# Linear attention and an MLP on one core: windows 3 to 5 back to chunks of 128, and a reordered beginning

## The chip, the cores and the metric

The kernel runs on one core of a Trainium2 chip. The metric is the device time of one execution in microseconds; the time before is the median of three runs, 218.67 us (218.31 to 218.92). The profile is of one such execution; its span, from the first to the last instruction, is 216.7 us.

## The reference

Inputs are q, k and v of shape (batch 4, heads 8, sequence 768, head size 64), one decay factor per head (lam, between 0.97 and 0.99), a LayerNorm weight of 512 and two MLP weights, 512 x 2048 and 2048 x 512, all in float32. Decaying linear attention is followed by an MLP with a residual:

```python
for b in range(nb):                                   # blocks of 64 positions
    intra = einsum('bhic,bhjc->bhij', qb, kb) * Dmask # Dmask = lam**(i-j) for i >= j, else 0
    intra = einsum('bhij,bhjd->bhid', intra, vb)
    inter = einsum('bhid,bhde->bhie', qb * lam_pow, kv_state)
    out[:, :, sl] = intra + inter
    kv_state = lam_block * kv_state + einsum('bhsd,bhse->bhde', kb * rev_pow, vb)
x  = out, heads side by side                          # (4, 768, 512)
xn = (x - mean) / sqrt(var + 1e-6) * g_ln
result = x + relu(xn @ w_ch1) @ w_ch2
```

The block of the reference is only a way to compute it: any block length gives the same values.

## The kernel before

Work goes in 12 windows of 256 positions; window u is batch u % 4, third u // 4 of the sequence. Each window has two halves of 128 rows (`ab`), and makes one group of 256 rows for the MLP: eight steps of the first product (`m1`, 8 matmuls of 256 columns each), then eight of the second (`m2`, 4 of 512 columns). TensorE takes the attention of later windows between these steps.

q is scaled by powers of lam and v by inverse powers, so that a plain 0/1 mask stands for the decay within a chunk. The constant LB parts the windows in two kinds. Below LB a chunk has 128 positions; two neighbouring positions lie on one partition, so that a load has rows of 512 bytes. From LB on a chunk has 64 positions, rows have 256 bytes, and a load is two transfers:

```python
    XB = 3
    LB = 3
    ...
    def source(src, u, hs):
        cc, b = divmod(u, B)
        return src[b, hs, cc * W:(cc + 1) * W, :].rearrange("h (p j) d -> p h (j d)", j=2)

    def fill(got, name, u, hs):
        src = dict(k=k, q=q, v=v)[name]
        if u < LB:
            nc.sync.dma_start(got[:, hs], source(src, u, hs))
            return
        cc, b = divmod(u, B)
        for j in range(2):
            nc.sync.dma_start(got[:, hs, j * D:(j + 1) * D],
                              src[b, hs, cc * W + j * C:cc * W + (j + 1) * C, :].rearrange("h p d -> p h d"))
```

The attention of a window in chunks of 128: `kv` (32 matmuls of 64 columns, the state's new terms), `scores` (two halves of 16 matmuls of 128 columns), `mask`, `av` (64 matmuls of 64 columns), `inter` (up to twice 16 matmuls with the carried state). In chunks of 64: `kv64` (32), `scores64` (32 of 64 columns), `mask64` (half as many elements), `av64` (32), `inter` as above, and two more sums for the states in between.

```python
    def scores(u, hf, early=False):
        ...                                      # sc: two PSUM tiles, of tag "mm" if early, else of tag "sc" (2 buffers)
        for i in range(2):
            for jk in range(2):
                for ab in range(2):
                    for e in range(2):
                        nc.tensor.matmul(sc[e][half[ab], i, jk, :], lhsT=kT[half[e], 2 * hf + i, jk, half[ab]],
                                         rhs=qT[half[e], 2 * hf + i, :, half[ab]], ...)

    def av(u, pairs, chunks=(0, 1)):
        ...
        for p in pairs:
            for e in range(2):
                for j in range(2):
                    for jq in range(2):
                        for ab in chunks:
                            nc.tensor.matmul(s["po"][ab][half[jq], 2 * p + e, :],
                                             lhsT=s[f"mA{p // 2}"][half[ab], e, p % 2, j, half[jq]],
                                             rhs=s["vb"][half[ab], 2 * p + e, j], ...)

    def av64(u):
        ...
        for p in range(NP):
            for e in range(2):
                for j in range(2):
                    for ab in range(2):
                        nc.tensor.matmul(s["po"][ab][half[j], 2 * p + e, :], lhsT=s["mA"][half[ab], e, p, j],
                                         rhs=s["vb"][half[ab], 2 * p + e, j], ...)

    def mask_by_act(u, hf):                      # ScalarE copies the scores out, VectorE multiplies by the mask
        for e in range(2):
            nc.scalar.copy(s[f"mA{hf}"][:, e], s[f"sc{hf}"][e])
        ...
```

The transposed keys and queries of windows 0 to 2 come from TensorE (`transpose_pe`, copied out of PSUM by ScalarE or VectorE), those of later windows from the DMA (`transpose_dma`, on the sync queue); so it is with x^T, the MLP's input (`to_xT`). The sync queue issues in program order, and all loads, transposes and nearly all stores are on it.

The beginning, up to the first MLP tile:

```python
    lam_b = const.tile([128, H], F32)
    nc.scalar.dma_start(lam_b, lam[None, :].to_broadcast([128, H]))
    load_window(0, parts=2)
    nc.scalar.dma_start(g_one, moe_g_ln[None, :])
    ...
    g_all = ps.tile([128, DM], F32, tag="po1", name="g_all")
    nc.tensor.matmul(g_all, lhsT=ones, rhs=g_one, start=True, stop=True)   # spreads the LayerNorm weight
    nc.scalar.activation(lnlam, lam_b, ACT.Ln)
    nc.scalar.activation(lam_q[:, :, 0], lnlam, ACT.Exp, scale=e_q)
    ...
    in_k(0, nc.vector, HA)
    transpose_pe(0, 0, (0, 1))
    keep_busy(1, "po0")                                                    # one filler matmul
    ...                                                                    # Exp: lam_v (2), lam_s (2), lam_p (2)
    in_q(0, nc.vector, HA)
    ...
    transpose_pe(0, 1, (0, 1))
    transpose_pe(0, 0, (2, 3), nc.vector)
    nc.scalar.copy(g_row, g_all)
    transpose_pe(0, 1, (2, 3))
    ...
    scores(0, 0)
    mask(0, 0)
    scores(0, 1, early=True)
    mask_by_act(0, 1)
    kv(0)
    ...                                          # state, av, inter, norm of window 0
    transpose_pe(1, 0, (0, 1), nc.vector)
    transpose_pe(1, 0, (2, 3), nc.vector)
    to_xT(0, 0)
    inter(0, 1)
    norm(0, 1, early=True)
    m1a.tile(0, 0)                               # first MLP tile
    to_xT(0, 1)
    ...
```

The later part is a list of MLP steps (`plan`), with attention steps hung behind given numbers; step 22 is the first of group 2, and a group has 16 steps (38 is the first of group 3, 54 of group 4, 70 of group 5):

```python
    add(11, (open_window, 3), (in_k, 3, nc.scalar), (in_q, 3, nc.gpsimd))
    add(12, (s4, 2), (make_keep64,), (in_v, 3, nc.gpsimd))
    add(12, (transpose_dma, 3, 0), (to_xT, 2, 0), (transpose_dma, 3, 1), (to_xT, 2, 1))
    for name in "kqv":
        add(12, (load_one, 4, name))
    ...
    add(22, (load_one, 5, "k"))
    add(22, (first64, 3))                        # kv64, scores64, masks and states of window 3
    add(26, (transpose_dma, 4, 0), (transpose_dma, 4, 1), (load_one, 5, "q"))
    add(28, (wind_up, 3), (p4, 3), (load_one, 5, "v"))
    add(32, (first64, 4))
    ...
    for j in range(5, NU):
        at = 55 + 16 * (j - 6)
        ...
        add(at + 2, (X, j), (p4, j - 1))         # rest of window j - 1, first half of window j
```

Of the kernel before, what the change touches and what calls it, by code (L numbers as in the profile page):

```python
# [16 lines left out]
def kernel(  # L17
# [11 lines left out]
    nc = tc.nc  # L29
# [23 lines left out]

    half = [slice(0, 64), slice(64, 128)]
    XB = 3
    LB = 3

    def mm_tile(shape, dtype, name):
        return ps.tile(shape, dtype, tag="mm", bufs=4, name=name)
# [43 lines left out]
    def load_w2(c):  # L103
        nc.gpsimd.dma_start(w2[c], moe_w_ch2[c * W2K * 128:(c + 1) * W2K * 128, :].rearrange("(k p) d -> p k d", p=128))

    lam_b = const.tile([128, H], F32)
    nc.scalar.dma_start(lam_b, lam[None, :].to_broadcast([128, H]))
    load_window(0, parts=2)
# [38 lines left out]
    eps_t = const.tile([128, 1], F32)  # L147
    nc.vector.memset(eps_t, eps)

    e_q = const.tile([128, 1], F32)  # L150
    nc.vector.tensor_copy(e_q, io_i)
    nc.vector.tensor_scalar(e_q[half[1]], e_q[half[1]], float(-C), None, op0=ALU.add)
# [7 lines left out]

    ones = const.tile([1, 128], F32)
    nc.vector.memset(ones, 1.0)
    g_all = ps.tile([128, DM], F32, tag="po1", name="g_all")
    nc.tensor.matmul(g_all, lhsT=ones, rhs=g_one, start=True, stop=True)  # L164

    lnlam = const.tile([128, H], F32)
    nc.scalar.activation(lnlam, lam_b, ACT.Ln)
    lam_q = const.tile([128, H, 2], F32)
# [26 lines left out]
    def in_k(u, eng, hs=ALL):  # L195
        src = qkv_in[u]["k"][:, hs].rearrange("p (a e) j d -> p a e j d", e=2)
        dst = part(0, st[u]["kq"], hs)
        for j in range(2):
            (eng.copy if eng is nc.scalar else eng.tensor_copy)(dst[:, :, :, j], src[:, :, :, j])  # L199
# [27 lines left out]
    def transpose_dma(u, a):  # L227
        s = st[u]
        if "kqT" not in s:
            s["kqT"] = wk.tile([128, 2, NP, 2, 128], BF16, tag="kqT", bufs=3, name="kqT")  # L230
        nc.sync.dma_start_transpose(s["kqT"][:, a].rearrange("p b j t -> p (b j) t"),
                                    s["kq"][:, a].rearrange("p b j e d -> p (b j e d)"))

    def scores(u, hf, early=False):

# [24 lines left out]
    def mask_by_act(u, hf):  # L260

        s = st[u]
        for e in range(2):
            nc.scalar.copy(s[f"mA{hf}"][:, e], s[f"sc{hf}"][e])
        kp = keep_h.rearrange("p a b t -> p a (b t)")
        for e in range(2):
            m = s[f"mA{hf}"][:, e]
            nc.vector.tensor_tensor(m, m, kp[:, None, :, :].to_broadcast([128, 2, 2, 128]), op=ALU.mult)

    def kv(u, tag="mm"):  # L270

# [170 lines left out]
    def to_xT(u, ab):  # L442
        s = st[u]
        t = 2 * u + ab
        g = group_of[t]
        i = t - groups[g][0]
        if i == 0:
            xT_of[g] = gp.tile([128, KA, GT * 128], BF16, tag="xT", bufs=3, name="xT")
        dst = xT_of[g][:, :, i * 128:(i + 1) * 128]
        if u >= 2:  # L450
            nc.sync.dma_start_transpose(dst, s["xc"][:, ab])
        else:
            xt = mm_tile([128, KA, 128], BF16, "xt")
# [145 lines left out]
    nc.vector.tensor_copy(e_p[:, 0:1], io_p)  # L599
    nc.vector.tensor_scalar(e_p[:, 1:2], e_p[:, 0:1], -1.0, None, op0=ALU.mult)  # L600
    for i in range(2):
        nc.scalar.activation(lam_p[:, i], lnlam, ACT.Exp, scale=e_p[:, i:i + 1])
    in_q(0, nc.vector, HA)
    behind(qkv_in[0]["k"][:, 0, 0, 0:1])
    load_w1(0)
# [9 lines left out]
    scores(0, 0)  # L615
# [40 lines left out]
    transpose_pe(1, 1, (2, 3))  # L656
# [45 lines left out]
    def first64(u):  # L702
        kv64(u)
        scores64(u)
        mask64(u, 0)
        states64(u, 0)
        mask64(u, 1)
        states64(u, 1)

    def s0(u):  # L710
        kv(u, "po")
# [15 lines left out]
    def wind_up(u):  # L727


        s = st[u]  # L730
        if u < LB:
            av(u, range(NP))
        else:
            av64(u)
        inter(u, 0, fence=False)
        qT = s["kqT"][:, 1]
        has = [s["S"][ab][1] is not None for ab in range(2)]
        rest = [ps.tile([128, H, D], F32, tag="sc", bufs=2, name=f"rest{ab}") if has[ab] else None for ab in range(2)]
# [3 lines that stand above are left out]
                    ab = 1 - e  # L742
                    if s["S"][ab][jq] is not None:
                        nc.tensor.matmul(rest[ab][half[jq], 2 * p + e, :], lhsT=qT[half[e], p, jq, half[ab]],
                                         rhs=s["S"][ab][jq][half[e], p, :],
                                         start=(p == 0), stop=(p == NP - 1), skip_group_check=True)
        s["x"] = xp.tile([128, 2, DM], F32, tag="x", name="x")
        s["mv"] = xp.tile([128, 2, 2], F32, tag="mv", name="mv")
        s["xc"] = wk.tile([128, 2, DM], BF16, tag="xc", name="xc")
        for ab in range(2):  # L750
            x, xh = s["x"][:, ab], s["x"][:, ab].rearrange("p (a e d) -> p a e d", e=2, d=D)
            nc.scalar.copy(x, s["po"][ab].rearrange("p h d -> p (h d)"))
            if has[ab]:

                odd = xh[:, :, 1 - ab]
                rows = slice(0, 128) if s["S"][ab][0] is not None else half[1]
                nc.vector.tensor_tensor(odd[rows], odd[rows], rest[ab].rearrange("p (a e) d -> p a e d", e=2)[rows, :, 1 - ab], op=ALU.add)
# [100 lines left out]
    add(6, (s2, 2))  # L858
    add(8, (s0, 2))
    add(10, (s3, 2))  # L860
    add(11, (open_window, 3), (in_k, 3, nc.scalar), (in_q, 3, nc.gpsimd))
    add(12, (s4, 2), (make_keep64,), (in_v, 3, nc.gpsimd))
    add(12, (transpose_dma, 3, 0), (to_xT, 2, 0), (transpose_dma, 3, 1), (to_xT, 2, 1))
    for name in "kqv":
        add(12, (load_one, 4, name))
    add(15, (rstd_of, 2))
    add(22, (load_one, 5, "k"))
    add(22, (first64, 3))
    add(23, (open_window, 4), (in_q, 4, nc.gpsimd), (in_v, 4, nc.gpsimd))
    add(25, (in_k, 4, nc.vector))  # L870
    add(26, (transpose_dma, 4, 0), (transpose_dma, 4, 1), (load_one, 5, "q"))
    add(28, (wind_up, 3), (p4, 3), (load_one, 5, "v"))
    add(28, (open_window, 5), (in_k, 5, nc.gpsimd))
    add(32, (first64, 4))
    add(32, (in_q, 5, nc.gpsimd), (in_v, 5, nc.gpsimd))
    add(34, (rstd_of, 3), (transpose_dma, 5, 0), (transpose_dma, 5, 1))
    for j in range(5, NU):
        at = 55 + 16 * (j - 6)
        if j > 5:
            for n, name in zip((20, 19, 18) if j == 6 else (23, 21, 19), "kqv"):  # L880
                add(at - n, (load_one, j, name))
            add(at - 13, (p0, j))
            add(at - 8, (transpose_dma, j, 0), (transpose_dma, j, 1))
        add(at + 2, (X, j), (p4, j - 1))
        add(at + 9, (rstd_of, j - 1))
    add(151, (wind_up, NU - 1), (p4, NU - 1))
    add(159, (rstd_of, NU - 1))
# [32 lines left out]
```

## Time and profile before

| | before |
|---|---|
| time, median of 3 | 218.67 us |
| span in the profile | 216.7 us |
| TensorE clock granted, mean of the span | 0.991 |
| DMA: bytes moved, mean rate | 37.13 MB, 171 GB/s |
| packets under 512 bytes, of all | 86961 of 103502 |

Times in the profile are microseconds from the span's start. PE is TensorE's matmuls, PEld its weight loads, DVE VectorE, ACT ScalarE, POOL GpSimd, SP the sync engine; a q behind a name means that engine's DMA issues. L484 is line 484 of the kernel: L484 is the first MLP product, L522 the second, L327 `scores64`, L164 the spread of the LayerNorm weight. TensorE's matmuls overlap, so a single one's duration is longer than the distance to the next: the rate is read from how long a run of them takes. An "issue" wait is one for which the profile shows no releaser.

### The profile page before, as it was taken

To read this page: it belongs to the slowest core of one execution; us is meant where nothing else is said; L and a number is where in the kernel's file an instruction comes from. 1 tells how busy PE (TensorE), PEld (TensorE's weight loads), DVE (VectorE), ACT (ScalarE), POOL (GpSimd) and SP (SyncE) were. 2 spreads that over 40 slices of the span, in tenths; PEclk is the share of its full clock that TensorE was granted. 3 is DMA by queue.
4 is the path that set the end of the run, shared out by engine and by line. 5 is a ranking of instruction groups with operands and counts; after the bars stand their busy time and mean duration, and the time that the engine had idled before them with its cause. 6 is when DMAs were issued, how large, how long until landed. Compare 5 with 4: busy or idle time off the path is not lost.

```text
span 216.7 us, 6491 instructions
## 1 busy us (share of the span) xinstructions
PE 199.6 (92%) x2796; PEld 137.4 (63%) x2811; DVE 102.5 (47%) x226; ACT 87.7 (40%) x167; POOL 81.1 (37%) x116
## 2 busy tenths in 40 slices
PE   2989899999991999999998999999999999999992
PEld 0468688444861486586575585684784874865862
DVE  2678452464852629338247246266174192532011
ACT  4766678140550046064063063262360460641610
POOL 4749049053372558418219129037055020000000
PEclk9999999999999799999999999999999999999999
DMA  4999999997989999999898799999987611320304
GB/s 122 291 271 209 225 267 167 224 208 150 211 256 220 154 222 238 197 176 228 166 221 196 145 235 182 147 219 208 208 194 150 146 23 32 101 48 0 100 0 97
DMA packets 103502, 37.13 MB, mean 171 GB/s; under 512 B 86961, under 2 KB 100529, under 8 KB 103474
## 3 DMA queue, kind: packets, MB, share of 16 engines
q1 hardware_dynamic: 98944, 32.39, 73.8%
q0 software_dynamic: 4224, 4.19, 12.1%
q8 instruction: 22, 0.36, 0.8%
q10 hardware_dynamic: 306, 0.14, 0.3%
q14 instruction: 6, 0.05, 0.1%
HBM read 27.27 MB, written 6.29 MB: 155 GB/s over the span
## 4 chain that ended last, share of the span: by engine, by line
PE 83%; DMA 5%; ACT 3%; DVE 3%; issue 2%; SPq 1%; POOL 0%; ACTq 0%
PE pm L522 36%; PE pm L484 34%; DMA kin<-in_k_dram 2%; PE pm1t L496 2%; PE pm2h L513 2%; DMA kqT<-kq 1%; PE sc L327 1%; PE po L380 1%; SPq L550 1%; DMA g_one<-in_moe_g_ln_dram 1%; PE po L406 1%; PE pk L346 1%; PE tp L224 1%; PE g_all L164 1%; ACT kqT L225 1%
## 5 line engine op out<-in xcount | busy, mean ns | idle before, releaser
L487 ACT ACTIVATE hT<-pm 128x512 bf16<-128x512 f32 x92 | 55.0, 601 | 94.0 <-PE pm L484 94.0
L484 PE MATMUL pm<-xT,w 128*128 128x256 bf16 x736 | 85.6, 273 | 1.0 <-issue 1.0
L522 PE MATMUL pm<-w,hT 128*128 128x512 bf16 x353 | 81.9, 382 | 1.2 <-issue 0.5
L484 PEld LDWEIGHTS <-w 128*128 128x128 bf16 x736 | 70.3, 98 | 12.4 <-issue 1.2
L522 PEld LDWEIGHTS <-hT 128*128 128x128 bf16 x368 | 35.8, 99 | 41.0 <-issue 1.4
L543 DVE SCALAR_TENSOR_TENSOR o<-pm,rstd,x 128x512 f32<-128x512 f32 x23 | 17.3, 750 | 48.1 <-PE pm L522 47.9
L287 POOL TENSOR_TENSOR Sn<-Stmp,lam_s 128x256 bf16<-128x256 f32 x17 | 10.5, 620 | 67.4 <-DVE Stmp L365 62.4
L210 POOL TENSOR_TENSOR kq<-qin,lam_p 128x512 bf16<-128x512 f32 x18 | 18.4, 1046 | 2.1 <-ACT kq L199 2.1
L216 POOL TENSOR_TENSOR vb<-vin,lam_p 128x1024 bf16<-128x1024 f32 x9 | 17.1, 1898 | 4.3 <-DMA vin<-in_v_dram 4.1
L435 DVE SCALAR_TENSOR_TENSOR xc<-po,mv,g_row 128x512 bf16<-128x512 f32 (+1 forms) x22 | 15.3, 701 | 1.7
L333 DVE TENSOR_TENSOR mA<-sc,keep 128x512 bf16<-128x512 f32 x18 | 12.3, 681 | 5.0 <-PE sc L327 5.0
L417 DVE COPY seen<-po 128x8 f32<-128x8 f32 x17 | 2.2, 161 | 25.5 <-PE po L406 25.5
L428 ACT COPY x<-po 128x512 f32<-128x512 f32 x16 | 8.7, 588 | 10.9 <-PE po L406 5.6
L430 DVE BATCH_NORM_STATS2 stats<-x 128x6 f32<-128x512 f32 x16 | 11.0, 684 | 0.8 <-ACT x L428 0.8
L199 POOL CAST kq<-kin 128x512 bf16<-128x512 f32 (+1 forms) x16 | 9.2, 603 | 4.2 <-DMA kin<-in_k_dram 4.2
L327 PE MATMUL sc<-kqT 64*64 64x64 bf16 x288 | 4.6, 199 | 4.7 <-DMA kqT<-kq 4.7
L362 DVE TENSOR_TENSOR Smid<-pk,Sn 128x256 f32<-128x256 f32 x17 | 7.2, 424 | 1.7
L257 DVE TENSOR_TENSOR mA<-sc,keep 128x512 bf16<-128x512 f32 x8 | 5.2, 686 | 5.6 <-PE sc L247 5.6
L370 POOL CAST Sm<-Smid 128x256 bf16<-128x256 f32 x18 | 7.4, 410 | 1.0 <-DVE Smid L362 1.0
L406 PE MATMUL po<-Sn,kqT 64*64 64x64 bf16 x172 | 7.0, 199 | 0.0
L327 PEld LDWEIGHTS <-kqT 64*64 64x64 bf16 x288 | 3.7, 111 | 4.8 <-issue 4.8
L365 DVE TENSOR_TENSOR Stmp<-pk,Smid 128x256 f32<-128x256 f32 x14 | 5.9, 424 | 0.7
(99 smaller groups left out, 152.8 us busy)
## 6 DMA issues: line engine op xcount, KB each, us to landing
out_dram<-o SPq DMA_DIRECT2D x22, 256.0 KB, 4.7
kin<-in_k_dram SPq DMA_DIRECT2D x20, 256.0 KB, 4.3
qin<-in_q_dram SPq DMA_DIRECT2D x20, 256.0 KB, 5.4
vin<-in_v_dram SPq DMA_DIRECT2D x20, 256.0 KB, 5.2
w<-in_moe_w_ch_dram POOLq DMA_DIRECT2D x8, 512.0 KB, 8.8
kin<-in_k_dram SPq DMA_DIRECT2D x2, 512.0 KB, 6.5
qin<-in_q_dram SPq DMA_DIRECT2D x2, 512.0 KB, 8.9
vin<-in_v_dram SPq DMA_DIRECT2D x2, 512.0 KB, 9.1
```

What stands on the lines that cost most here:

```text
L199: (eng.copy if eng is nc.scalar else eng.tensor_copy)(dst[:, :, :, j], src[:, :, :, j])
L210: eng.tensor_tensor(dst[:, :, :, j], src[:, :, :, j], lq[:, :, :, j:j + 1].to_broadcast([128, n, 2, D]), op=ALU.mult)
L216: eng.tensor_tensor(st[u]["vb"][:, hs], qkv_in[u]["v"][:, hs], lv.to_broadcast([128, n, 2, D]), op=ALU.mult)
L287: eng.tensor_tensor(dst, src, lam_s[:, :, None].to_broadcast([128, NP, D]), op=ALU.mult)
L327: nc.tensor.matmul(s["sc"][e][half[ab], p, j, :], lhsT=kT[half[e], p, j, half[ab]], rhs=qT[half[e], p, j, half[ab]], start=(p == 0 and j = ...
L333: nc.vector.tensor_tensor(s["mA"][:, e], s["sc"][e], keep64[:, None, None, :].to_broadcast([128, NP, 2, D]), op=ALU.mult)
L430: nc.vector.bn_stats(stats, po if early else x)
L435: nc.vector.scalar_tensor_tensor(xc[:, sl], in0=po[:, sl], scalar=mv[:, 0:1], in1=g_row[:, sl], op0=ALU.subtract, op1=ALU.mult)
L484: nc.tensor.matmul(pm[:, b, :], lhsT=w1[n // W2K][:, kk, (n % W2K) * 128:(n % W2K + 1) * 128], rhs=xT_of[g][:, kk, 0:N], start=(b == 0 and ...
L487: nc.scalar.activation(hT[:, u * NB:(u + 1) * NB, 0:N], pm, ACT.Relu)
L522: nc.tensor.matmul(acc[i], lhsT=hT[:, kk, i * 128:(i + 1) * 128], rhs=w2[kk // W2K][:, kk % W2K, :], start=(kk == 0), stop=(kk == KB - 1))
L543: nc.vector.scalar_tensor_tensor(o[:, ab], in0=a, scalar=rstd[:, ab:ab + 1], in1=x[:, ab], op0=ALU.mult, op1=ALU.add)
```

## The change

It does two things. Windows 3 to 5 are computed in chunks of 128 again (LB is 6 instead of 3), with their own placement in the step list: window 4 is loaded right behind window 3, window 5 some steps later, and each window's attention is spread over four places. This gives loads with longer rows, and other times for loads, transposes and the attention's matmuls.

The beginning is reordered: one activation table with logarithm and exponential is loaded at the start instead of two at first use; the exponentials run one after the other; the LayerNorm weight is spread after the first key transposes, and the filler matmul is left out; the second half of window 0's mask is split between VectorE and ScalarE; the first x^T is built in two PSUM banks, copied out by two engines; and window 1's key transposes stand behind the first MLP tile.

```diff
-    LB = 3
+    LB = 6
...
+    nc.scalar.preload_act_table_set("natural_log_exp_and_others")
     lam_b = const.tile([128, H], F32)
     nc.scalar.dma_start(lam_b, lam[None, :].to_broadcast([128, H]))
...
-    g_all = ps.tile([128, DM], F32, tag="po1", name="g_all")
-    nc.tensor.matmul(g_all, lhsT=ones, rhs=g_one, start=True, stop=True)
...
+    def mask_two_ways(u, hf):
+        s = st[u]
+        m = s[f"mA{hf}"][:, 1]
+        nc.scalar.copy(m, s[f"sc{hf}"][1])
+        mask(u, hf, (0,))
+        kp = keep_h.rearrange("p a b t -> p a (b t)")
+        nc.vector.tensor_tensor(m, m, kp[:, None, :, :].to_broadcast([128, 2, 2, 128]), op=ALU.mult)
...
-            xt = mm_tile([128, KA, 128], BF16, "xt")
-            for kk in range(KA):
-                nc.tensor.transpose(xt[:, kk, :], s["xc"][:, ab, kk * 128:(kk + 1) * 128], ident)
-            nc.scalar.copy(dst, xt)
+            n_x = 2 if t == 0 else 1
+            for i_x in range(n_x):
+                w = KA // n_x
+                xt = mm_tile([128, w, 128], BF16, "xt")
+                for kk in range(w):
+                    at = i_x * w + kk
+                    nc.tensor.transpose(xt[:, kk, :], s["xc"][:, ab, at * 128:(at + 1) * 128], ident)
+                (nc.vector.tensor_copy if i_x else nc.scalar.copy)(dst[:, i_x * w:(i_x + 1) * w], xt)
...
-    in_k(0, nc.vector, HA)
-    transpose_pe(0, 0, (0, 1))
-    keep_busy(1, "po0")
     for j in range(2):
         nc.scalar.activation(lam_v[:, :, j], lnlam, ACT.Exp, scale=e_v[:, j:j + 1])
     ...                                          # lam_s
+    in_k(0, nc.vector, HA)
+    transpose_pe(0, 0, (0, 1))
+    g_all = ps.tile([128, DM], F32, tag="po1", name="g_all")
+    nc.tensor.matmul(g_all, lhsT=ones, rhs=g_one, start=True, stop=True)
...
     transpose_pe(0, 1, (0, 1))
     transpose_pe(0, 0, (2, 3), nc.vector)
+    scores(0, 0)
+    transpose_pe(0, 1, (2, 3))
     nc.scalar.copy(g_row, g_all)
-    transpose_pe(0, 1, (2, 3))
+    for i in range(2):
+        nc.scalar.activation(lam_p[:, i], lnlam, ACT.Exp, scale=e_p[:, i:i + 1])
...
-    mask_by_act(0, 1)
+    mask_two_ways(0, 1)
...
-    transpose_pe(1, 0, (0, 1), nc.vector)
-    transpose_pe(1, 0, (2, 3), nc.vector)
     to_xT(0, 0)
     inter(0, 1)
     norm(0, 1, early=True)
     st[0]["tmp"] = state_sum(0, 1)
     m1a.tile(0, 0)
+    transpose_pe(1, 0, (0, 1), nc.vector)
+    transpose_pe(1, 0, (2, 3), nc.vector)
     to_xT(0, 1)
...
     load_window(3, after_pool=True)
+    load_window(4)
...
+    add(12, (s4, 2), (p4, 2), (p0, 3, nc.vector), (transpose_dma, 3))
+    for n, name in zip((14, 15, 16), "kqv"):
+        add(n, (load_one, 5, name))
+    add(17, (p0, 4))
+    add(25, (s1, 3))                              # s1: kv, scores half 0, states, masks
+    add(25, (transpose_dma, 4))
+    add(27, (s2, 3))                              # s2: scores half 1, masks
+    add(28, (p0, 5))                              # p0: k, q and v of a window to bf16, scaled
+    add(29, (s3, 3))                              # s3: av, first carry
+    add(30, (s4, 3), (p4, 3))                     # s4: second carry, norm; p4: x^T by DMA
+    for n, name in zip((30, 31, 32), "kqv"):
+        add(n, (load_one, 6, name))
...
+    add(37, (transpose_dma, 5))
+    add(38, (s1, 4))
+    add(39, (p0, 6))
+    add(40, (s2, 4))
+    add(42, (s3, 4))
+    add(44, (s4, 4), (p4, 4))
+    add(46, (transpose_dma, 6))
+    add(50, (s1, 5), (rstd_of, 4))
+    add(53, (s2, 5))
...
+            if j == 6:
+                add(at + 1, (X1, j))              # rest of window 5, states of window 6
+                add(at + 5, (X2, j), (p4, j - 1)) # scores and masks of window 6, end of window 5
+            else:
                 add(at + 2, (X, j), (p4, j - 1))
```

More of the change, by code (lines that the diff above doesn't have):

```diff
@@ L148 @@
     nc.vector.memset(eps_t, eps)
+    nc.vector.tensor_copy(e_p[:, 0:1], io_p)
+    nc.vector.tensor_scalar(e_p[:, 1:2], e_p[:, 0:1], -1.0, None, op0=ALU.mult)
     e_q = const.tile([128, 1], F32)
@@ L225, in transpose_pe, with transpose_dma @@
         (eng.tensor_copy if eng else nc.scalar.copy)(s["kqT"][:, a, pairs[0]:pairs[0] + n], tp)
-    def transpose_dma(u, a):
+    def transpose_dma(u):
         s = st[u]
[L229 to L232, printed above, removed]
+        s["kqT"] = wk.tile([128, 2, NP, 2, 128], BF16, tag="kqT", bufs=3, name="kqT")
+        for a in range(2):
+            nc.sync.dma_start_transpose(s["kqT"][:, a].rearrange("p b j t -> p (b j) t"),
+                                        s["kq"][:, a].rearrange("p b j e d -> p (b j e d)"))
     def scores(u, hf, early=False):
@@ L597 @@
         nc.scalar.activation(lam_s[half[e]], ln_p[half[e], :, e], ACT.Exp, scale=float(C))
+    in_k(0, nc.vector, HA)
+    transpose_pe(0, 0, (0, 1))
+    g_all = ps.tile([128, DM], F32, tag="po1", name="g_all")
+    nc.tensor.matmul(g_all, lhsT=ones, rhs=g_one, start=True, stop=True)
     nc.vector.tensor_tensor(lam_q[:, :, 1], lam_q[:, :, 0], lam_b, op=ALU.mult)
[L599 to L602, printed above, removed]
     in_q(0, nc.vector, HA)
@@ L614 @@
     in_v(0, nc.gpsimd, HB)
-    scores(0, 0)
     mask(0, 0)
     scores(0, 1, early=True)
-    mask_by_act(0, 1)
+    mask_two_ways(0, 1)
     kv(0)
@@ L700, in p0 @@
         in_v(u, nc.gpsimd)
[L702 to L708, printed above, removed]
     def s0(u):
@@ L755, in wind_up @@
                 odd = xh[:, :, 1 - ab]
-                rows = slice(0, 128) if s["S"][ab][0] is not None else half[1]
-                nc.vector.tensor_tensor(odd[rows], odd[rows], rest[ab].rearrange("p (a e) d -> p a e d", e=2)[rows, :, 1 - ab], op=ALU.add)
+                nc.vector.tensor_tensor(odd, odd, rest[ab].rearrange("p (a e) d -> p a e d", e=2)[:, :, 1 - ab], op=ALU.add)
             stats = wk.tile([128, 6], F32, tag="stats", name="stats")
@@ L860 @@
     add(10, (s3, 2))
[L861 to L865, printed above, removed]
-    add(15, (rstd_of, 2))
[L867 to L877, printed above, removed]
+    add(12, (s4, 2), (p4, 2), (p0, 3, nc.vector), (transpose_dma, 3))
+    for n, name in zip((14, 15, 16), "kqv"):
+        add(n, (load_one, 5, name))
@@ new lines @@
+    add(15, (rstd_of, 2))
+    add(17, (p0, 4))
[7 more added lines that the diff above has]
+        add(n, (load_one, 6, name))
+    add(34, (rstd_of, 3), (make_keep64,))
+    add(37, (transpose_dma, 5))
[5 more added lines that the diff above has]
+    add(46, (transpose_dma, 6))
@@ L878 @@
+    add(50, (s1, 5), (rstd_of, 4))
+    add(53, (s2, 5))
+    for j in range(6, NU):
         at = 55 + 16 * (j - 6)
-        if j > 5:
-            for n, name in zip((20, 19, 18) if j == 6 else (23, 21, 19), "kqv"):
+        if j > 6:
+            for n, name in zip((23, 21, 19), "kqv"):
                 add(at - n, (load_one, j, name))
             add(at - 13, (p0, j))
-            add(at - 8, (transpose_dma, j, 0), (transpose_dma, j, 1))
-        add(at + 2, (X, j), (p4, j - 1))
+            add(at - 8, (transpose_dma, j))
+        if j < LB:
+            add(at, (s1_s3, j))
+            add(at + 4, (s2_s4, j), (p4, j - 1))
+        else:
+            if j == 6:
+                add(at + 1, (X1, j))
+                add(at + 5, (X2, j), (p4, j - 1))
+            else:
+                add(at + 2, (X, j), (p4, j - 1))
```

## The prediction

> **What bounds the kernel now.** I read the busy shares first, then the chain that ended last, then TensorE's waits, then stretches cut where the chain changes, then the timelines of the sync queue and of ScalarE. The first line says that TensorE is the bound, and the second, the engines' shares of the chain, agrees:
>
> ```profile
> PE 199.6 (92%) x2796; PEld 137.4 (63%) x2811; DVE 102.5 (47%) x226; ACT 87.7 (40%) x167; POOL 81.1 (37%) x116
> ...
> PE 83%; DMA 5%; ACT 3%; DVE 3%; issue 2%; SPq 1%; POOL 0%; ACTq 0%
> ```
>
> So only two things can move the time: matmul work, and the 17.1 us (216.7 - 199.6) in which TensorE stands still. TensorE's waits (engine, line, releaser: sum, times, longest in us) name most of that idle time:
>
> ```profile
> PE sc L327 <- DMA kqT<-kq: 4.7, 1, 4.7
> PE g_all L164 <- DMA g_one<-in_moe_g_ln_dram: 4.1, 1, 4.1
> PE pm L484 <- issue: 1.0, 1, 1.0
> PE po L393 <- issue: 0.7, 1, 0.7
> ```
>
> The second is the wait for the first data. The first is one hole in mid-kernel. Stretches (start:end, length; busy us of the engines; granted clock, DMA share, GB/s) place it. The four below are window 2 with the second products of groups 0 and 1, then the stages of groups 2, 3 and 4:
>
> ```profile
> 37.86:53.83 15.97, 15.65 (x191) 7.47 (x193) 8.43 (x17) 3.10 (x6) 5.22 (x8) 1.00 1.01 192
> 53.83:76.16 22.33, 17.21 (x281) 11.50 (x281) 12.72 (x25) 6.05 (x11) 10.57 (x15) 0.92 1.06 212
> 76.16:91.52 15.36, 15.31 (x225) 10.47 (x225) 7.77 (x17) 6.05 (x11) 9.48 (x11) 1.00 1.08 218
> 91.52:106.88 15.36, 15.31 (x225) 10.46 (x225) 7.76 (x17) 6.05 (x11) 6.93 (x9) 1.00 1.03 191
> ```
>
> Group 2's stage takes 22.33 us, a normal one 15.36. The timelines of the sync queue (start, duration) and of TensorE, one after the other, show why:
>
> ```profile
> 58.60 3.32 SPq L550 DMA_DIRECT2D out_dram<-o  x4
> 61.96 2.39 SPq L75 DMA_DIRECT2D kin<-in_k_dram  x2
> 64.46 3.49 SPq L231 DMA_TRANSPOSE kqT<-kq  x2
> ...
> 70.00 0.65 PE L327 MATMUL sc<-kqT 64*64 64x64 bf16 x32 [4.73 <-DMA kqT<-kq]
> 70.98 5.18 PE L522 MATMUL pm<-w,hT 128*128 128x512 bf16 x19 [0.33 <-issue]
> ```
>
> Window 4's q and k were ready near 61.9, but their transposes stood behind four stores and window 5's k load; they landed at 69.9, when window 4's scores had been waiting since 65.3. Then 19 matmuls took 5.18 us, 273 ns each, against 216 ns in undisturbed stretches (6.64 us for 30, with gaps): 1.1 us more. The granted clock is 0.57 in 69 to 72 us and 0.86 in 72 to 75.
>
> **What the Trainium skill says.** "TensorE: Matmul & The Clock Gate", section "Part 1: The HAM clock gate", says that an idle window of about 3.4 us halves the clock until a busy one has passed. The 4.73 us hole and the granted clock after it agree. "DMA: Bandwidth & Descriptors", section "Why small descriptors are slow (HBM only)", gives a fixed overhead per packet. Here 512-byte rows, almost alone, moved at 298 GB/s (6 to 9 us) and 256-byte rows at 230 to 232 (42 to 48 us), so windows 3 to 5, which change to 512-byte rows, should load about a fifth faster. The same page, "Queues, rings and completion order", has descriptors consumed in ring order: window 4's transposes landed after 4.9 us at worst against a median of 3.3. "ScalarE: Activation LUTs", section "Table sets: the hidden batching unit", has one set with both logarithm and exponential. The trace has three loads of 1.28 us; two are for this pair.
>
> **Part 1, windows 3 to 5 go back to chunks of 128 (LB 3 to 6).** In the stretch of window 2, 64 second products cost 64 x 216 ns = 13.8 us of 15.97, so 2.17 us is attention: one half of the scores, states, products with v, and two short carry groups. The other half of the scores (0.35 us, in the chain at 36.54) makes 2.5 us per window. Windows 4 and 5 have full carries, some 0.15 us more. A window in chunks of 64 costs 15.36 - (64 x 109 ns + 32 x 216 ns = 13.9) = 1.45 us. The new placement is split over four places instead of one, at about 0.1 us each, which is already in the 2.5. I place the pieces by the new step list:
> - Group 2's stage: two products 13.9, all of window 3, 2.35: 16.3 us. Now 22.33.
> - Group 3's stage: all of window 4 and the scores and states of window 5, 3.8: 17.7 us. Now 15.36.
> - Group 4's stage: window 5's rest and window 6's first half, 1.85: 15.8 us. Now 15.36.
>
> Sum 49.8 against 53.05: **-3.3 us**. This is the hole with its slow clock (about 6.2 us) less about 3 us of extra small matmuls. It holds only if no such hole opens again.
>
> **Does the hole close?** Loads of window 4 are issued right behind window 3's (37 us instead of 52), window 5's at steps 14 to 16. At about 300 GB/s the 3.15 MB of windows 3 and 4 need 10.5 us from 39.8, where the last weights are in: done near 50.3. The transposes of window 2's x (xc ready at 48.4) then land near 53.5, just as group 2 needs them at 53.8. Window 4's key transposes go out at step 25, near 60 us, for scores at step 38, near 69. So the hole closes. The tight places: scores of window 3 (transposes near 56.5, wanted at 57.3); the second score half two steps (1.75 us) after the first, while the two score banks are freed by two masks of 0.68, two sums of 0.42 and a GpSimd scaling of 0.61 in sequence (some 0.3 us late, twice); and x^T of window 3, produced at step 30 for step 38. I put **+0.6 us** for these together.
>
> **Part 2, the beginning.** ScalarE's timeline is what counts here:
>
> ```profile
> 0.81 0.43 ACTq L107 DMA_DIRECT2D lam_b<-in_lam_dram  x1
> 1.28 0.53 ACTq L111 DMA_DIRECT2D g_one<-in_moe_g_ln_dram  x1
> 1.84 1.28 ACT L167 ACT_TABLE_LOAD   x1 [1.84 <-issue]
> 4.36 0.21 ACT L167 ACTIVATE lnlam<-lam_b 128x8 f32<-128x8 f32 x1 [1.23 <-DMA lam_b<-in_lam_dram]
> 4.58 1.28 ACT L169 ACT_TABLE_LOAD   x1
> 5.88 0.30 ACT L169 ACTIVATE lam_q<-lnlam,e_q 128x8 f32<-128x8 f32 x1
> ```
>
> The second load (1.28 us) goes, but the new one is issued ahead of the two small transfers on the same queue. If they wait for it, the decay row lands at about 5.65 instead of 4.36, and lam_q is ready at 6.2 as now: no gain. If not, lam_q is ready at 4.9, but q itself arrives only near 6. The spread of the LayerNorm weight (2.04 us on TensorE, now 4.14 to 6.18, in front of the first transposes) moves behind the first key transposes: these start at 5.65 instead of 6.18, but the first q transposes, now at 7.02 to 7.8, must wait for 6.2 + 2.04 = 8.24. The filler matmul (0.63) was in an idle place. From 8.24 on: q transposed 8.75, copied 9.4, first scores 9.45 to 10.1 (now 9.08), last q transposes behind them, copied 11.2, second scores at 11.25 (now 10.05). ScalarE then has the weight copy (0.58) and two exponentials (0.49) ahead of its mask copy; the last mask ends near 13.3 (now 12.3). The split x^T copy gives back 0.3 us. The first MLP tile starts near 16.4 instead of 15.84. Window 1's key transposes, now hidden in waits, then lie between that tile and the next: a few tenths more, partly hidden. I take **+0.7 us** for the whole beginning, and hold -0.7 to +1.3 possible, since TensorE may fill some of these gaps. The kernel stays bound by TensorE from there, so this shift reaches the end.
>
> **Sum.** 218.67 - 3.3 + 0.6 + 0.7 = 216.67, taken as 216.6 us.
>
> **Rivals.** (a) The hole returns elsewhere: for it, the sync queue issues in order and DMA is busy at a share of about 1 until 170 us; against it, loads are earlier, larger-grained, and now ahead of the stores. One new wait of 3 us with a slow clock would make 220 to 221. (b) The beginning becomes faster, with exponentials out of ScalarE's way and masks in parallel; for it, four ScalarE instructions now stand between the first two key and q copies (6.76 to 8.46 us). Then about 215.0, and 214 if the two "issue" waits also go, which name no releaser. (c) VectorE becomes the bound in group 3's stage: it gains two masks and loses two sums per window, about +0.5 us, and was busy 7.8 of 15.4 us; unlikely, and worth at most 1 us.
>
> **Range and chances.** The hole's size is measured, its closing likely (about 85%); the extra matmuls are known to about 0.7 us, the beginning to about 1 us. That gives 213.8 to 219.0. Faster by over 2% means below 214.3: it needs the beginning to gain as well, 0.17. Slower by over 2% means above 223.0, which needs a hole as long as the old one: 0.05.
>
> **What would show it.** The wait of scores for kqT is gone, and the clock stays at 1.00 from 54 to 107 us. Groups 2 to 4 take near 16.3, 17.7 and 15.8 us. The matmul count rises by 87 (96 more products with v, 8 fewer carries in window 3, the filler). One table load less. The first q transposes begin after g_all ends, near 8.2 us, and the first MLP tile after 16 us. Wrong it would be if TensorE waits over 1 us for xT or kqT, if the first tile comes before 15.5 us, or if the three stages sum to over 51.5 us.

## The result and the profile after

The changed kernel takes 215.74 us (median of 4 runs, 215.20 to 216.32), the kernel before beside it 218.79: a ratio of 0.986, 95% interval 0.983 to 0.990. In a later comparison (`after_again` below) the ratio was 0.980 (0.977 to 0.984). The kernel before varies more: its medians in the five comparisons were 218.8 to 221.0. So below, ratios to the kernel before are compared, and times only within one comparison.

The page of the changed kernel, its busy shares and the engines' shares of the chain that ended last:

```profile
PE 200.2 (94%) x2883; PEld 138.0 (64%) x2898; DVE 103.7 (48%) x226; ACT 84.8 (40%) x163; POOL 79.0 (37%) x111
...
PE 91%; DVE 3%; DMA 2%; ACT 2%; issue 1%; POOL 0%
```

TensorE has 87 matmuls more (2883 against 2796) and 0.6 us more busy time, and yet the span is 2.7 us shorter: idle time went from 17.1 to 13.8 us. TensorE's waits, longest first, show what is left:

```profile
PE tp L224 <- POOL seen_p L592: 5.8, 1, 5.8
PE xt L468 <- DVE xc L444: 1.3, 2, 1.1
PE sce L247 <- ACT kqT L225: 0.7, 1, 0.7
PE pm L535 <- issue: 0.3, 2, 0.2
```

The 4.7 us for kqT (the transposed keys and queries) are gone, and nothing took their place. All that remains above 0.3 us lies in the first 17 us; the longest, 5.8 us, is the wait for window 0's keys, of which the weight's spread filled 2 us before. The stretches that answer to those of before (columns as there): window 2, then the stages of groups 2, 3, 4, then group 5:

```profile
38.06:55.01 16.95, 16.63 (x200) 8.34 (x203) 10.46 (x19) 2.52 (x5) 9.44 (x9) 1.00 1.18 259
55.01:71.33 16.32, 16.27 (x242) 10.79 (x241) 8.33 (x17) 6.24 (x11) 6.73 (x11) 1.00 0.95 226
71.33:88.95 17.62, 17.37 (x320) 11.38 (x320) 10.65 (x22) 5.94 (x11) 7.50 (x9) 1.00 1.05 172
88.95:104.73 15.78, 15.73 (x257) 10.82 (x259) 8.74 (x19) 6.01 (x11) 6.88 (x9) 1.00 0.89 185
104.73:120.10 15.37, 15.32 (x226) 10.48 (x225) 7.77 (x17) 6.05 (x11) 6.88 (x9) 1.00 1.09 191
```

The clock is 1.00 in all of them. The first stretch starts one step of the first product earlier in the work than the one shown of before; measured from the same step, 36.88 to 53.83, that one is 16.95 us long too. The books of the two traces:

| stretch | before | after | difference |
|---|---|---|---|
| start to group 2's first product | 53.83 | 55.01 | +1.18 |
| groups 2, 3, 4 | 53.05 | 49.72 | -3.33 |
| group 5 | 16.42 | 15.37 | -1.05 |
| group 6 | 15.22 | 15.22 | 0.00 |
| group 7 | 15.22 | 15.71 | +0.49 |
| rest | 62.96 | 62.97 | +0.01 |
| span | 216.70 | 214.00 | -2.70 |

Groups 5 to 7 run the same code in both. Their -0.56 us is mostly a matter of "issue" waits, 0.97 us in group 5 before and 0.3 us in group 7 after, which name no releaser and lie elsewhere in each trace. So the change itself is worth about -3.3 in the middle and, on this one pair of traces, +1.2 in the beginning.

The sync queue, where the hole came from. The first line is window 4's k load before, at 51.9 us; the others are of the changed kernel: the same load at 41.7, x^T of window 2, window 4's transposes:

```profile
51.91 1.20 SPq L75 DMA_DIRECT2D kin<-in_k_dram  x2
...
41.66 2.38 SPq L71 DMA_DIRECT2D kin<-in_k_dram  x1
...
47.79 3.64 SPq L460 DMA_TRANSPOSE xT<-xc  x2
...
61.38 5.00 SPq L231 DMA_TRANSPOSE kqT<-kq  x2
```

These transposes serve scores that begin at 72.4, six microseconds after the last of them was issued. And the beginning, ScalarE's first instructions, then TensorE's:

```profile
0.81 1.28 ACT L106 ACT_TABLE_LOAD   x1 [0.81 <-PEq L924]
0.84 0.43 ACTq L108 DMA_DIRECT2D lam_b<-in_lam_dram  x1
...
6.43 2.07 PE L611 MATMUL g_all<-g_one,ones 1*128 1x512 f32 x2
8.44 1.03 PE L224 MATMUL tp<-ident,kq 128*128 128x128 bf16 x8
...
16.64 1.89 PE L509 MATMUL pm1t<-xT,w 128*128 128x128 bf16 x16
```

The table load did not hold up the issue of the transfers behind it. The q transposes stood behind the weight's spread until 8.44. The first MLP tile began at 16.64 instead of 15.84, the second at 20.48 instead of 18.87.

### The profile page after: what moved, and what is told of

Same layout as the page of the kernel before. It is cut to its first block, busy times and chain, and to the rows that moved or that the text cites. A ratio compares the mean times of both kernels' runs of the same rounds, so it can differ in the third digit from the quotient of the medians.

```text
span 214.0 us, 6637 instructions
## 1 busy us (share of the span) xinstructions
PE 200.2 (94%) x2883; PEld 138.0 (64%) x2898; DVE 103.7 (48%) x226; ACT 84.8 (40%) x163; POOL 79.0 (37%) x111
## 4 chain that ended last, share of the span: by engine, by line
PE 91%; DVE 3%; DMA 2%; ACT 2%; issue 1%; POOL 0%
PE pm L497 37%; PE pm L535 37%; PE pm1t L509 2%; DMA kin<-in_k_dram 2%; PE po L402 2%; PE sc L247 2%; PE tp L224 2%; PE pm2h L526 2%; PE po L415 2%; PE po L389 1%; PE pk L290 1%; DVE xc L444 1%; PE g_all L611 1%; DVE stats L439 1%; PE sc L336 1%
## 5 line engine op out<-in xcount | busy, mean ns | idle before, releaser
L556 DVE SCALAR_TENSOR_TENSOR o<-pm,rstd,x 128x512 f32<-128x512 f32 x23 | 17.1, 747 | 43.2 <-PE pm L535 43.2
L444 DVE SCALAR_TENSOR_TENSOR xc<-po,mv,g_row 128x512 bf16<-128x512 f32 (+1 forms) x24 | 16.8, 705 | 1.8
L257 DVE TENSOR_TENSOR mA<-sc,keep 128x512 bf16<-128x512 f32 x20 | 13.1, 683 | 6.1 <-PE sc L247 6.0
L439 DVE BATCH_NORM_STATS2 stats<-x 128x6 f32<-128x512 f32 x18 | 12.4, 687 | 4.0 <-ACT x L437 3.9
L210 POOL TENSOR_TENSOR kq<-qin,lam_p 128x512 bf16<-128x512 f32 x12 | 12.3, 1042 | 0.0
L216 POOL TENSOR_TENSOR vb<-vin,lam_p 128x1024 bf16<-128x1024 f32 x6 | 11.4, 1896 | 1.9 <-DMA vin<-in_v_dram 1.8
L216 POOL TENSOR_TENSOR vb<-vin,lam_v 128x1024 bf16<-128x1024 f32 (+1 forms) x7 | 11.6, 1660 | 1.1 <-DMA vin<-in_v_dram 1.1
L210 POOL TENSOR_TENSOR kq<-qin,lam_q 128x512 bf16<-128x512 f32 x10 | 10.3, 1044 | 4.6 <-DMA qin<-in_q_dram 4.6
L224 PE MATMUL tp<-ident,kq 128*128 128x128 bf16 x48 | 5.4, 272 | 5.8 <-POOL seen_p L592 5.8
L224 PEld LDWEIGHTS <-kq 128*128 128x128 bf16 x48 | 4.2, 124 | 7.6 <-DVE kq L199 5.8
L342 DVE TENSOR_TENSOR mA<-sc,keep 128x512 bf16<-128x512 f32 x12 | 8.2, 680 | 1.4 <-PE sc L336 1.4
L474 ACT ACTIVATE std<-mv,eps_t 128x2 f32<-128x2 f32 x12 | 3.6, 299 | 6.5 <-DVE mv L440 6.5
```

The costliest lines, as they stand in the source:

```text
L210: eng.tensor_tensor(dst[:, :, :, j], src[:, :, :, j], lq[:, :, :, j:j + 1].to_broadcast([128, n, 2, D]), op=ALU.mult)
L216: eng.tensor_tensor(st[u]["vb"][:, hs], qkv_in[u]["v"][:, hs], lv.to_broadcast([128, n, 2, D]), op=ALU.mult)
L257: nc.vector.tensor_tensor(s[f"mA{hf}"][:, e], s[f"sc{hf}"][e], kp[:, None, :, :].to_broadcast([128, 2, 2, 128]), op=ALU.mult)
L439: nc.vector.bn_stats(stats, po if early else x)
L444: nc.vector.scalar_tensor_tensor(xc[:, sl], in0=po[:, sl], scalar=mv[:, 0:1], in1=g_row[:, sl], op0=ALU.subtract, op1=ALU.mult)
L556: nc.vector.scalar_tensor_tensor(o[:, ab], in0=a, scalar=rstd[:, ab:ab + 1], in1=x[:, ab], op0=ALU.mult, op1=ALU.add)
```

## The experiments

Each trace below is of one execution, which can lie up to some 2 us from the median of its kernel. My theory after the result: the middle is worth 3.3 us because window 4's inputs come early, and the beginning costs 1.2. Rivals: the longer rows alone close the hole, or the order on the sync queue alone; and the beginning costs nothing, since something other than TensorE sets when group 2 can start.

**1. The change without its beginning, and the beginning alone.** `mid_only` is the changed kernel with all of the reordered beginning undone; `begin_only` is the kernel before with the new beginning. The core of the edit (for `mid_only`; the other way round for `begin_only`):

```diff
-    nc.scalar.preload_act_table_set("natural_log_exp_and_others")
+    g_all = ps.tile(...); nc.tensor.matmul(g_all, lhsT=ones, rhs=g_one, ...)   # at its old place
     ...   # exponentials, filler, mask by ScalarE, x^T in one bank, window 1's key transposes: as before
```

> The changed kernel with the old beginning: windows 3 to 5 in chunks of 128 and their placement stay, all of the reordered beginning is undone. My theory (the middle gains 3.3 us, the new beginning costs about 1.2 us[...]): first MLP tile at 15.8 us, group 2's first product near 53.8, stages of groups 2 to 4 again 49.7 us together, time 214.3 to 214.9, ratio to the kernel before 0.980 to 0.983. Rival (the beginning is paid back by what follows, so that it costs nothing): 215.7, ratio 0.986.

> The kernel before with only the new beginning. My theory: first MLP tile near 16.6, all later work 1.2 us later, time near 220.0, ratio 1.005. Rival (the hole at window 4's scores ends when the DMA lets it end, not when TensorE arrives, so it swallows a later start): the wait for kqT falls from 4.7 to about 3.5 us and the time stays at 218.8, ratio 1.000. Second rival (the beginning is a gain): below 218.3.

`mid_only`: 216.06 us against 219.3, ratio 0.986 (0.979 to 0.993). `begin_only`: 220.25, ratio 1.0057 (1.0028 to 1.0086), that is +1.2 us (+1.0 by the medians). So on the kernel before the new beginning costs what I reckoned for this run, and the hole did not swallow it (its wait fell only from 4.7 to 4.2 us). On the changed kernel taking it out brought nothing that these four runs show. The chain of `mid_only` (start, length, what) says what TensorE met instead:

```profile
8.14 12.84 DMA vin<-in_v_dram
21.05 1.91 POOL vb L216
23.00 0.45 PE pk L290 x32
...
23.00 0.45 PE L290 MATMUL pk<-vb,kq 64*64 64x64 bf16 x32 [0.49 <-POOL vb L216]
```

Its second MLP tile came early, at 19.14, but window 1's v load, issued at 8.1, landed only near 21; scaled by GpSimd it was ready at 23.0. TensorE had other work until 22.5 and stood 0.5 us for it, as the last line (of its timeline) shows; the expectation of `mid_only2` below counts 2 us, which is too much. At group 2 it stood again, 0.6 us for x^T.

**2. The same question with more runs.** `after_again` is the changed kernel unaltered, `mid_only2` is `mid_only` again, on one chip.

> The changed kernel once more, unaltered, beside the next one: 0.986 of the kernel before, 49.7 us for the stages of groups 2 to 4. It tells whether the old beginning (next run) is worth anything here, which one run of four times could not.

> The changed kernel with the old beginning, again, in more rounds. In its first trace TensorE came to window 1's state matmuls at 21 us and stood until 23.0, because window 1's v load had landed only at 21.0 and its scaling took 1.9 us. Floor theory (that landing sets the start of what follows, so an earlier first MLP tile gains nothing): the same time as the unaltered changed kernel within 0.4 us, the wait for vb again in the trace. Cost theory (the new beginning costs 1.2 us also here): 1 us or more faster than the unaltered one.

216.04 us (215.39 to 216.55) and 216.58 us (214.35 to 216.95): ratios 0.9804 (0.9769 to 0.9840) and 0.9812 (0.9770 to 0.9854). No gain from the old beginning shows in the changed kernel. A gain of 1.2 us would be a ratio near 0.975, below both intervals; a smaller one is not excluded. So the time fits the floor theory (the floor is the time before which a load has not landed, however early TensorE comes) better than the cost theory, but the place of the wait was mostly another than I expected: 0.2 us for window 1's v, and at the start of group 2

```profile
PE pm L493 <- DMA xT<-xc: 1.1, 1, 1.1
```

x^T of window 2 stands on the sync queue behind window 4's loads, and these behind window 3's. The first of window 3's loads waits for GpSimd, which comes to it only after issuing the weights and scaling window 2's q and v. That load went out at 36.4 us in `after_again` and at 37.2 in `mid_only2`, and x^T at 47.9 and 49.3. In all fourteen traces of this study the load went out between 36.4 and 38.1 us, whether the first MLP tile began at 15.8 or at 16.6. Among the changed kernel and its variants it even went out later with the old beginning (37.2 to 38.1, four traces) than with the new one (36.4 to 37.0, six traces, `g_early` among them); why is not shown. (In `mid_only2` itself the first tile began only at 16.58, after a wait of 0.9 us for window 1's keys, and the second at 19.60, still 0.9 us ahead of `after_again`. Group 2 began at 55.3 against 54.9.)

**3. The weight's spread back in front.** `g_early` undoes one part of the beginning in the changed kernel:

```diff
+    g_all = ps.tile(...); nc.tensor.matmul(g_all, ...)     # behind the memset of ones
     ...
     transpose_pe(0, 0, (0, 1))
-    g_all = ps.tile(...); nc.tensor.matmul(g_all, ...)
```

> The changed kernel with the spread of the LayerNorm weight back in its old place, ahead of the first key transposes. My theory (that matmul pair of 2.07 us stands in front of the first q transposes): key transposes later (near 6.8 us), first q transposes near 7.4 instead of 8.44, first MLP tile 0.6 to 0.9 us earlier than 16.64, time near 215.0, ratio near 0.983. Rival (ScalarE's order, not the matmul's place, sets the beginning): first MLP tile within 0.2 us of 16.64, ratio 0.986.

```profile
5.15 2.04 PE L167 MATMUL g_all<-g_one,ones 1*128 1x512 f32 x2 [5.15 <-DMA g_one<-in_moe_g_ln_dram]
7.12 1.46 PE L227 MATMUL tp<-ident,kq 128*128 128x128 bf16 x12
...
15.81 1.89 PE L512 MATMUL pm1t<-xT,w 128*128 128x128 bf16 x16
```

The first MLP tile began at 15.81 us instead of 16.64: the place of that matmul pair is what moved it, as reckoned. The time was 216.0 us, ratio 0.987 (0.979 to 0.995): no gain that four runs can show. The trace does not fit a floor, though: it has no wait for window 1's v or for x^T, group 2 began at 54.3 instead of 54.9, and the span is 213.3 us, against 214.0 and 213.9 in the two traces of the unaltered kernel. In this one execution most of the shift did reach the end.

**4. Order alone.** `hole_order`, the kernel before with window 5's k load behind window 4's transposes:

```diff
-    add(22, (load_one, 5, "k"))
-    add(26, (transpose_dma, 4, 0), (transpose_dma, 4, 1), (load_one, 5, "q"))
+    add(26, (transpose_dma, 4, 0), (transpose_dma, 4, 1), (load_one, 5, "k"), (load_one, 5, "q"))
```

> The kernel before, where the k load of window 5 is issued behind window 4's key and query transposes instead of ahead of them. Order theory: the transposes go out at 62 us and land near 65.5 to 66.5, the wait of window 4's scores for kqT falls from 4.7 to below 1.2 us, the clock stays at 1.00 there; but x^T of window 3 and window 5's inputs come later, so that part of it comes back as a new wait of 1 to 3 us, and the time is 214 to 217. Rate theory (the DMA engines are full there, the order matters little): the wait stays above 3.5 us and the time within 1 us of 218.8.

220.54 us, ratio 1.0058 (1.0031 to 1.0084). Neither figure was met: the wait fell to 3.3 us, not below 1.2. The sync queue of this kernel, stores and then the transposes:

```profile
59.72 3.43 SPq L550 DMA_DIRECT2D out_dram<-o  x4
63.26 3.97 SPq L231 DMA_TRANSPOSE kqT<-kq  x2
```

The transposes had no k load in front and still took from 63.3 to 67.2 to issue. The wait is 1.4 us shorter, but the scores themselves began only 0.4 us earlier (69.6 against 70.0): this trace ran some 1.1 us late by then, on TensorE and on the queue, after early waits for window 1's v (1.3 us) and for a weight (0.8) that the trace of the kernel before did not have. So order is worth at most 1.4 of the 4.7 us. New waits for window 5's v (0.8) and x^T of window 3 (0.6), both issued over 1 us later than before, gave that back.

**5. Early loads without long rows, and long rows without early loads.** `early4` is the kernel before with window 4's loads behind window 3's; `late4` is the changed kernel with them back at step 12:

```diff
     load_window(3, after_pool=True)
+    load_window(4)                           # early4; late4 takes this line away
...
-    for name in "kqv":                       # early4; late4 adds these lines
-        add(12, (load_one, 4, name))
```

> The kernel before with one thing of the change: window 4's loads are issued right behind window 3's instead of at step 12 (rows stay at 256 bytes, chunks at 64). Load-time theory (the hole comes from window 4's loads being late, so that stores, loads and transposes pile up on the sync queue): the wait of scores for kqT is at most 1 us, the slow clock after it is gone; the 256-byte rows may bring x^T of window 2 late, a wait of up to 2 us ahead of group 2; time 213 to 217. Row theory (only the longer rows help): the wait for kqT stays above 3 us, or the x^T wait takes its whole place; time 218 or more.

> The changed kernel with window 4's loads back at step 12, behind the transposes of window 3. Load-time theory: window 4's inputs land near 60 us, its transposes near 68 to 70, TensorE waits for them or for x^T of window 3 for 1 to 4 us: 217 to 220. Row theory (the rows of 512 bytes alone close the hole): no wait above 0.5 us, time within 0.5 us of the unaltered changed kernel.

`early4`: 224.4 us, ratio 1.018 (1.013 to 1.023). The wait for kqT is gone, but

```profile
PE pm L484 <- DMA xT<-xc: 8.4, 4, 7.0
```

7.0 us of it at the start of group 2: with 256-byte rows the loads of windows 3 and 4 held the sync queue until 53.9 us (47.7 in the changed kernel), and the two parts of x^T of window 2, behind them and alternating with window 3's transposes, went out at 56.4 and 59.0. That is the row theory's second form, with a larger size than I gave it. Part of it may be the order, which no run parts from the row length: in the changed kernel both parts of x^T stand ahead of window 3's transposes.

`late4`: 221.18 us, ratio 1.0066 (1.0041 to 1.0090). Here it is x^T of window 3 that comes late:

```profile
PE pm L497 <- DMA xT<-xc: 4.1, 1, 4.1
```

Group 2's stage, with this wait at its end, takes 20.65 us instead of 16.32, and the clock is slow after it (0.51 in 75 to 78 us). So long rows alone close the wait for kqT, and so do early loads alone, but each opens another for x^T, and the kernel is slower than before. In the placements tried it takes both: window 4's loads must be out of the way before x^T of window 2 is ready, and with short rows they were not. LB = 6 brings long rows, longer chunks and the spread placement together; no run parts these three.

**6. Moving one load off x^T's way.** `mid_v4late` is `mid_only` with window 4's v load behind x^T of window 2:

```diff
-    load_window(4)
+    load_one(4, "k"); load_one(4, "q")
...
-    add(12, (s4, 2), (p4, 2), (p0, 3, nc.vector), (transpose_dma, 3))
+    add(12, (s4, 2), (p4, 2), (load_one, 4, "v"), (p0, 3, nc.vector), (transpose_dma, 3))
```

> The changed kernel with the old beginning, and window 4's v load moved behind x^T of window 2 on the sync queue (its k and q loads stay early). Floor theory (with the old beginning TensorE arrives at group 2 earlier, but x^T of window 2 stands behind window 4's loads on the sync queue, so the start is lost there): the wait for xT at the start of group 2 (1.1 us) goes, group 2 starts near 54.2 instead of 55.3, time 0.7 to 1.2 us below the changed kernel with the old beginning alone: about 215.5, ratio near 0.977 if the kernel before stands at 220. Rival (the early start is lost at window 1's v, not here): group 2 starts after 55 and the time is as before, 216.5.

216.29 us, ratio 0.986 (0.981 to 0.991): no gain. The x^T wait halved (0.5 us), but this trace, of the slowest of six executions (217.59 us), waited 1.1 us for window 1's q, 1.4 us for its v, and then 1.1 us for window 3's kqT, now behind the moved load. Group 2 began at 54.9, not at the expected 54.2. The rival came closer: more than one load sets the floor.

**7. One window fewer in chunks of 128.** `lb5` sets LB to 5, so that window 5 is in chunks of 64 again; `best` adds this to `mid_v4late`; `lb5_order` puts window 5's transposes ahead of window 6's loads:

```diff
-    LB = 6
+    LB = 5
-    add(42, (s3, 4))
-    add(44, (s4, 4), (p4, 4))
+    add(42, (X1, 5))
+    add(44, (X2, 5), (p4, 4))
-    add(37, (transpose_dma, 5))
+    add(35, (transpose_dma, 5))              # lb5_order: at step 30, behind p4 of window 3
     ...                                      # s1 and s2 of window 5 left out; window 6 by X
```

> The changed kernel with window 5 alone in chunks of 64 again (its loads in 256-byte rows, its attention hung with window 4's second half at steps 42 and 44). From the stage lengths a window in chunks of 128 costs TensorE about 1.0 us more than one in chunks of 64: stages of groups 3 and 4 fall from 17.7 and 15.7 to 17.0 and 15.4, time about 1.0 us below the changed kernel, 215.0. Rival (256-byte rows and the later key transposes of window 5 bring a wait back): a wait for kqT or vb of over 1 us at window 5, time at or above 216.

> Both steps of the other two together: old beginning, window 4's v load behind x^T of window 2, window 5 in chunks of 64. If both theories hold they add: 2.0 us below the changed kernel with the old beginning, 214.5, below both kernels. If either wait returns, 215.5 to 216.5.

> The changed kernel with window 5 in chunks of 64 as before, but window 5's key and query transposes issued ahead of window 6's loads instead of behind them. Order theory: they go out near 71 instead of 78 us, the wait of window 5's scores for kqT (2.6 us) goes, and groups 3 and 4 fall from 20.0 + 15.4 to 17.0 + 15.4; the wait for x^T of window 3 (1.3 us, from window 5's loads in 256-byte rows ahead of it) stays: 216 to 217.5. Rate theory: the kqT wait stays above 1.5 us or moves to window 6, 219 or more.

`lb5`: 220.68 us, ratio 1.0047 (1.0013 to 1.0081); the rival was right. In its trace, of the fastest of ten executions (218.62 us), group 4 took 15.37 us as reckoned, but group 3 took 19.98 instead of 17.0, and group 2 17.73:

```profile
PE sc L336 <- DMA kqT<-kq: 2.6, 1, 2.6
PE pm L497 <- DMA xT<-xc: 1.3, 1, 1.3
```

`best`: 220.59 us, ratio 1.0034 (1.0006 to 1.0062), where 214.5 was hoped for. `lb5_order`: 222.97 us, ratio 1.0115 (1.0026 to 1.0203). The kqT wait did go, and another came: window 6's loads were now late, GpSimd met window 6's inputs in program order ahead of window 5's state, and the PSUM tile that this state's sum still had to read was not free for the MLP. (2.9 us for x^T of window 3 and 1.8 us of "issue" came on top.) GpSimd's timeline (with the wait in brackets), then TensorE's:

```profile
87.61 1.90 POOL L216 TENSOR_TENSOR vb<-vin,lam_p 128x1024 bf16<-128x1024 f32 x1 [2.26 <-DMA vin<-in_v_dram]
89.47 0.61 POOL L296 TENSOR_TENSOR Sn<-Stmp,lam_s 128x256 bf16<-128x256 f32 x1
...
90.59 0.58 PE L535 MATMUL pm<-w,hT 128*128 128x512 bf16 x1 [2.48 <-DVE Smid L371]
```

No version that I ran is shown to beat the changed kernel.

## Why the prediction was right

- **The middle, -3.3 us: right, and for the reckoned reasons.** The three stages were to take 16.3, 17.7 and 15.8 us and took 16.32, 17.62 and 15.78. The costs of one window read from the stretches of before carried over to within 0.1 us, and the clock stayed at 1.00.
- **The cause of the hole: right in kind, wrong in its parts.** I put window 4's transposes behind "four stores and window 5's k load". The k load is worth at most 1.4 of 4.7 us (`hole_order`). What counts is when window 4's load goes out and how fast it moves; each without the other only moves the wait to x^T (`early4` 1.018, `late4` 1.007).
- **The small waits, +0.6 us: too much.** None of the three tight places cost anything in the changed kernel; all waits between 17 and 105 us come to some 0.8 us, and none of them is one of these three. They were real, though: x^T of window 3, one of the three, is where `late4`, `lb5` and `lb5_order` stopped, and x^T of window 2, which I had landing "just as group 2 needs them", is where the runs with the old beginning, or with short rows and early loads, did.
- **The beginning, +0.7 us: its inner working right, its effect wrong.** The alternative that I left standing for ScalarE (transfers not held up by the table load) was the true one, though the first activation on the decay row began at 5.16 in this trace, at 4.44 in `after_again` and at 4.36 before. First q transposes at 8.44 (8.24 reckoned), first tile at 16.64 (16.4). The second tile, 1.6 us later than before, was underestimated: window 1's key transposes in front of it were not hidden. The weak step is "The kernel stays bound by TensorE from there, so this shift reaches the end". It does on the kernel before (`begin_only`, +1.2 us). In the changed kernel the old beginning is no faster (`mid_only2`, 0.9812 against 0.9804): in its traces TensorE waits for window 1's inputs and window 2's x^T, which come no earlier. `g_early`, whose trace has no such wait, speaks against this as a rule, so what the new beginning costs in the changed kernel stays open, somewhere between nothing and about 1 us.
- **The total: 216.6 against 215.74.** The sum's three terms were -3.3, +0.6 and +0.7. Measured in the pair of traces they were -3.3, 0 and +1.2, and -0.6 us more came from "issue" waits that differ between traces, which I had left out of the sum and kept as an upside. That the total came so close is partly luck: 0.6 us too much in the second term and 0.5 too little in the third cancel.

What stays open: a part-by-part price of the beginning against a DMA that is less loaded was not tried, nor long rows, longer chunks and the spread placement one by one. Why the kernel before varies more from comparison to comparison (218.8 to 221.0) than the changed one (215.7 and 216.0) is not shown.

## What to carry to other kernels

When the bounding engine has one long hole, price the closing by stages: the work that the fix adds, the hole, and the slow clock after it; here that came out within 0.1 us per stage. A transfer queue that issues in order has to be read as a whole: moving one load, one transpose or one row length alone opened a new wait elsewhere in all six tries (`hole_order`, `early4`, `late4`, `mid_v4late`, `lb5`, `lb5_order`). Before counting a gain or loss in the beginning, look for a load that lands later than the engine arrives: there it can be lost again.

## What I had not expected of the hardware

- A DMA issue on ScalarE's queue went out at 0.84 us while the 1.28 us table load that precedes it in the program, begun at 0.81, was still running.
- The slow clock came after a TensorE wait of 3.3 us too (`hole_order`: 19 matmuls of 512 columns in 5.21 us, granted clock 0.51 in 69 to 72 us). After a wait of 2.6 us (`lb5`) it did not: 1.00, and 32 of them in 7.07 us. "TensorE: Matmul & The Clock Gate", section "Part 1: The HAM clock gate", of the Trainium skill names an idle window of about 3.4 us. The waits here don't give a sharp border: `lb5_order` has the slow clock after a wait of 2.9 us (8 matmuls of 256 columns in 1.87 us, against 1.03 to 1.05 in other traces), and again between two waits of 1.8 and 2.5 us (0.50 in 88 to 92 us). The first wait of each run, 4.1 to 5.8 us for the first data, shows 1.00 in every trace.

```profile
74.45 1.87 PE L497 MATMUL pm<-xT,w 128*128 128x256 bf16 x8 [2.88 <-DMA xT<-xc]
```

- With loads alone on the sync queue, the longer rows reached 301 GB/s (42 to 45 us in the changed kernel; 268 and 274 in the 3 us before and after), against 232 with the short ones (42 to 45 us before): at best 23% less time for the same bytes, where a fifth had been reckoned.
